# A chunked state-space layer gated with a feed-forward layer: filler tiles, the scan's PSUM copy and the start-up reordered

## Chip, cores and metric

One core of a Trainium2 chip. The metric is the device time in microseconds (us) of one execution. The kernel before takes 337.68 us (median of 4 runs, 336.47 to 340.53). Engines are called as the profile calls them: PE (TensorE), DVE (VectorE), ACT (ScalarE), POOL (GpSimd), SP (SyncE, which issues the transfers here).

## The reference

Two branches read the same x of 2048 rows and 640 columns and are mixed by a gate per row. `A` is a diagonal complex recurrence over 2048 rows with 640 states; `B` is a feed-forward layer with 1728 hidden units.

```python
def _A_ref(x, Lambda_re, Lambda_im, B_re, B_im, C_re, C_im, log_dt, Dskip):
    ...
    Lam_bar = jnp.exp(dt * Lam)
    B_bar = ((Lam_bar - 1.0) / Lam)[:, None] * Bmat
    Bu = jnp.einsum("bld,pd->blp", x + 0j, B_bar)
    ...
    for t in range(L):
        h = Lam_bar[None, :] * h + Bu[:, t, :]
        hs.append(h)
    hseq = jnp.stack(hs, 1)
    y = 2.0 * jnp.einsum("blp,dp->bld", hseq, Cmat).real + x * Dskip[None, None, :]
    return y

def _B_ref(x, w1, w2):
    h = jnp.einsum("bsd,df->bsf", x, w1)
    h = _silu(h)
    return jnp.einsum("bsf,fd->bsd", h, w2)

g = _sigmoid((x * gate_w).sum(-1, keepdims=True))
return g * a + (1 - g) * b
```

## The kernel before

The recurrence is cut into 16 chunks of 128 rows. For chunk c, PE computes `Bu` (U in PSUM) and the gate; DVE multiplies U by decaying powers (`do_V`); PE sums V over time with a triangular matrix (`do_CS`); the sums go to SBUF with the state at the end of the previous chunk (`hpf`) added (`do_CScopy`); DVE multiplies by growing powers (`do_S`), and PE multiplies S by the scaled C matrix (`do_y`). Chunk c needs `hpf` of chunk c-1, so this is a cycle. FFN2 of a chunk (`do_b`) and the hidden tiles of FFN1 (`ffn1_tile`: five matmuls, a sigmoid on ACT, a multiply on DVE) have nothing to do with the cycle and can fill gaps; tiles placed in the loop are called fillers. There are 56 tiles, 14 for each 512 rows.

The PSUM tensor `pbig` has eight banks of 512 columns. CS and y share columns from 2048 on (banks 4 to 6). The narrow FFN2 output (`B2C`, bank 6) shares a bank with the end of CS. The wide FFN2 output is bank 7. In the loop every filler uses bank 0.

```python
NPRE = 2 * FT                 # 28 tiles before the loop
...
def ffn1_tile(n):
    ...
    pr = (n % 4) if n < NPRE else 0      # bank of the tile
    ...
def do_CScopy(c):
    for t in range(10):
        ...                              # bias: zcol, or hpf of the chunk before
        def fn(a, t=t, bias=bias):
            return a.activation(CSsb[:, 128 * t:128 * (t + 1)],
                                pbig[:, R3C + 128 * t:R3C + 128 * (t + 1)],
                                ACTF.Identity, bias=bias)
        ...
# start-up: transfers in the order  x (5), w1 (1), B (10), w2 (2), C (10),
# then the parameter vectors and matrices on DVE, mixed with tiles,
# then the scaling of C (10 on ACT, 10 on DVE) mixed with tiles, then:
do_Bu(0); ...; do_V(0); tiles(2); do_CS(0); do_CScopy(0); do_S(0)
tiles(NPRE)
...
for c in range(NCH):
    fl = list(filler.get(c, []))         # chunks 4 to 11: 4, 3, 4, 3, ... tiles
    if c + 1 < NCH:
        do_Bu(c + 1); do_gate(c + 1); do_Ucopy(c + 1); do_gsig(c + 1)
        do_V(c + 1)
    if fl:
        ffn1_tile(fl.pop(0))
    do_b(c); do_t2(c)
    if fl:
        ffn1_tile(fl.pop(0))
    do_y(c); do_t1(c); do_out(c)
    for rest in fl:
        ffn1_tile(rest)
    if c + 1 < NCH:
        do_CS(c + 1); do_CScopy(c + 1); do_S(c + 1)
```

Of the kernel before, what the change touches and what calls it, by code (L numbers as in the profile page):

```python
# [11 lines left out]
D_MOD = 640  # L12
# [7 lines left out]
NPRE = 2 * FT  # L20
# [14 lines left out]
def _ptile(t):  # L35
    if t < 4:
        return t
    if t < 8:
        return t - 4
    return 4  # L40

# [113 lines left out]
def bass_gated_mix__ssm_conv_s5__dense_activation_silu__prompt_kernel(  # L155
# [19 lines left out]
    with ExitStack() as ctx:  # L175
# [11 lines left out]
        CTraw = sb("CTraw", [128, 10, D_MOD], bf16)  # L187
# [23 lines left out]
        T2s = sb("T2s", [128, 2 * P_ST], bf16)  # L211
        hpf = [sb(f"hpf{i}", [128, 10], f32) for i in range(2)]
        zcol = sb("zcol", [128, 1], f32)
# [3 lines left out]
        sig = [sb(f"sig{i}", [128, 512], bf16) for i in range(2)]  # L217
        ident = sb("ident", [128, 128], bf16)
        LT = sb("LT", [128, 128], bf16)
        halfpi = sb("halfpi", [128, 1], f32)  # L220
        stage = sb("stage", [5, 5 * 128], bf16)
# [25 lines left out]
        g_x = _DmaGroup(sem("s_x"), "DMA_x")  # L247
        g_w1 = _DmaGroup(sem("s_w1"), "DMA_w1")
# [20 lines left out]
        for kt in range(KT):  # L269
            dma(xT[:, kt, :], A_x[0, :, kt * 128:(kt + 1) * 128], g_x, writes=["xT"], transpose=True)  # L270
        dma(w1[:, :, :], B_w1[:, :].rearrange("(kt p) f -> p kt f", p=128), g_w1, writes=["w1"])
        for kt in range(KT):
            dma(BT[:, kt, 0:P_ST], A_B_re[:, kt * 128:(kt + 1) * 128], g_bt, writes=["BT"], transpose=True)
            dma(BT[:, kt, P_ST:2 * P_ST], A_B_im[:, kt * 128:(kt + 1) * 128], g_bt, writes=["BT"],
                transpose=True)
        dma(w2[:, 0:FT - 1, :],
            B_w2[0:(FT - 1) * 128, :].rearrange("(kt p) d -> p kt d", p=128), g_w2, writes=["w2"])
        dma(w2[0:64, FT - 1, :], B_w2[(FT - 1) * 128:F_FF, :], g_w2, writes=["w2"])
        for t5 in range(KT):
            dma(CTraw[:, t5, :], A_C_re[:, t5 * 128:(t5 + 1) * 128], g_ct, writes=["CTraw"],  # L280
                transpose=True)
            dma(CTraw[:, KT + t5, :], A_C_im[:, t5 * 128:(t5 + 1) * 128], g_ct, writes=["CTraw"],
                transpose=True)
# [15 lines left out]
        pool(lambda g: g.memset(zcol[:, :], 0.0), writes=["zcol"])  # L299

        def ffn1_tile(n):
# [3 lines left out]
            pr = (n % 4) if n < NPRE else 0  # L305
            pc = 512 * pr
            tok = f"hTp{pr}"
            for kt in range(KT):
# [5 lines left out]
                kw = dict(reads=["w1", "xT"], writes=rb(pc, pc + 512))  # L314
# [5 lines left out]
            def fs(a, rows_f=rows_f, n=n, pc=pc):  # L320
                return a.activation(sig[n % 2][0:rows_f, :], pbig[0:rows_f, pc:pc + 512], ACTF.Sigmoid)  # L321
            S.op(ACT, fs, reads=[tok] + rb(pc, pc + 512), writes=[f"sig{n % 2}"])
            def fm(v, rows_f=rows_f, n=n, buf=buf, ft=ft, pc=pc):
                return v.tensor_tensor(hT[buf][0:rows_f, ft, :], pbig[0:rows_f, pc:pc + 512],  # L324
                                       sig[n % 2][0:rows_f, :], ALU.mult)
            S.op(DVE, fm, reads=[tok, f"sig{n % 2}"] + rb(pc, pc + 512),
# [71 lines left out]
        S.op(DVE, lambda v: v.tensor_copy(Ere[:, :, 0:1], cols[:, I_LRE, 0:KT].unsqueeze(2)),  # L398
             reads=[f"col{I_LRE}"], writes=["Ere"])
        S.op(DVE, lambda v: v.tensor_copy(Eim[:, :, 0:1], cols[:, I_LIM, 0:KT].unsqueeze(2)),  # L400
             reads=[f"col{I_LIM}"], writes=["Eim"])
        S.op(DVE, lambda v: v.tensor_copy(col(I_PRA), col(I_LRE)), reads=[f"col{I_LRE}"], writes=[f"col{I_PRA}"])
        S.op(DVE, lambda v: v.tensor_copy(col(I_PIA), col(I_LIM)), reads=[f"col{I_LIM}"], writes=[f"col{I_PIA}"])
        pcur = [I_PRA, I_PIA]
        pnxt = [I_PRB, I_PIB]

        def e_round(r):
            nonlocal pcur, pnxt
            w = 1 << r
            pre, pim = pcur  # L410
            def fA(v, w=w, pre=pre):
                return v.tensor_tensor(tAb[:, :, 0:w], Ere[:, :, 0:w], bc_col(pre, w), ALU.mult)
            def fB(v, w=w, pim=pim):
                return v.tensor_tensor(tBb[:, :, 0:w], Eim[:, :, 0:w], bc_col(pim, w), ALU.mult)
            def fC(v, w=w, pim=pim):
                return v.tensor_tensor(tCb[:, :, 0:w], Ere[:, :, 0:w], bc_col(pim, w), ALU.mult)
            def fD(v, w=w, pre=pre):
                return v.tensor_tensor(tDb[:, :, 0:w], Eim[:, :, 0:w], bc_col(pre, w), ALU.mult)
# [4 lines left out]
            S.op(DVE, lambda v, w=w: v.tensor_tensor(Ere[:, :, w:2 * w], tAb[:, :, 0:w], tBb[:, :, 0:w], ALU.subtract),  # L423
                 reads=["tA", "tB"], writes=["Ere"])
            S.op(DVE, lambda v, w=w: v.tensor_tensor(Eim[:, :, w:2 * w], tCb[:, :, 0:w], tDb[:, :, 0:w], ALU.add),
                 reads=["tC", "tD"], writes=["Eim"])
            if r < 6:
# [5 lines left out]
                S.op(DVE, lambda v, pin=pin: v.tensor_scalar_mul(col(pin), col(I_DEN), 2.0),  # L433
                     reads=[f"col{I_DEN}"], writes=[f"col{pin}"])
                pcur, pnxt = pnxt, pcur

        for r in range(7):
            e_round(r)

        S.op(DVE, lambda v: v.tensor_copy(Aa[:, 0:4, :], Ere[:, 0:4, :]), reads=["Ere"], writes=["Aa"])  # L440
        S.op(DVE, lambda v: v.tensor_copy(Aa[:, 4:8, :], Ere[:, 0:4, :]), reads=["Ere"], writes=["Aa"])
        S.op(DVE, lambda v: v.tensor_copy(Aa[:, 8, :], Ere[:, 4, :]), reads=["Ere"], writes=["Aa"])
        S.op(DVE, lambda v: v.tensor_copy(Aa[:, 9, :], Ere[:, 4, :]), reads=["Ere"], writes=["Aa"])
        tiles(2)
        S.op(DVE, lambda v: v.tensor_scalar_mul(An[:, 0:4, :], Eim[:, 0:4, :], -1.0), reads=["Eim"], writes=["An"])
        S.op(DVE, lambda v: v.tensor_scalar_mul(An[:, 8, :], Eim[:, 4, :], -1.0), reads=["Eim"], writes=["An"])
        S.op(DVE, lambda v: v.tensor_copy(An[:, 4:8, :], Eim[:, 0:4, :]), reads=["Eim"], writes=["An"])
        S.op(DVE, lambda v: v.tensor_copy(An[:, 9, :], Eim[:, 4, :]), reads=["Eim"], writes=["An"])
        tiles(2)
        S.op(DVE, lambda v: v.tensor_tensor(dd1[:, :, :], Ere[:, :, :], Ere[:, :, :], ALU.mult),  # L450
             reads=["Ere"], writes=["dd1"])
        S.op(DVE, lambda v: v.tensor_tensor(dd2[:, :, :], Eim[:, :, :], Eim[:, :, :], ALU.mult),
             reads=["Eim"], writes=["dd2"])
        tiles(1)
        S.op(DVE, lambda v: v.tensor_tensor(dd3[:, :, :], dd1[:, :, :], dd2[:, :, :], ALU.add),
             reads=["dd1", "dd2"], writes=["dd3"])
        S.op(DVE, lambda v: v.reciprocal(dd1[:, :, :], dd3[:, :, :]), reads=["dd3"], writes=["dd1"])
        tiles(2)
        S.op(DVE, lambda v: v.tensor_tensor(Rre_b[:, :, :], Ere[:, :, :], dd1[:, :, :], ALU.mult),
             reads=["Ere", "dd1"], writes=["Rre_b"])  # L460
        S.op(DVE, lambda v: v.tensor_tensor(Rimn_b[:, :, :], Eim[:, :, :], dd1[:, :, :], ALU.mult),
             reads=["Eim", "dd1"], writes=["Rimn_b"])
        tiles(1)
# [12 lines left out]
        for t in range(10):  # L476
# [11 lines left out]
            if t % 2 == 1:  # L488
                tiles(1)
        for kt in range(KT):  # L490
            def fn(v, kt=kt):
                return v.tensor_scalar(Ddiag[:, kt, :], ident[:, :],
                                       cols[:, I_D, kt:kt + 1], None, ALU.mult)
            S.op(DVE, fn, reads=["ident", f"col{I_D}"], writes=["Ddiag"])
        tiles(2)

        def retile(t5):
            return t5 if t5 < 4 else 8

        def imtile(t5):  # L500
            return t5 + 4 if t5 < 4 else 9

        for t5 in range(KT):
            rt, it = retile(t5), imtile(t5)
            def fa(a, t5=t5):
                return a.activation(T1s[:, 0:D_MOD], CTraw[:, t5, :], ACTF.Copy,
                                    scale=cols[:, I_K2IM, t5:t5 + 1])
            S.op(ACT, fa, reads=["CTraw", f"col{I_K2IM}"], writes=["T1s"])
            def fb(v, t5=t5, it=it):
                return v.scalar_tensor_tensor(CTT[:, it, :], CTraw[:, KT + t5, :],  # L510
                                              cols[:, I_NK2RE, t5:t5 + 1], T1s[:, 0:D_MOD],
                                              ALU.mult, ALU.subtract)
            S.op(DVE, fb, reads=["CTraw", f"col{I_NK2RE}", "T1s"], writes=["CTT"])
            def fc(a, t5=t5):
                return a.activation(T2s[:, 0:D_MOD], CTraw[:, KT + t5, :], ACTF.Copy,
                                    scale=cols[:, I_K2IM, t5:t5 + 1])
            S.op(ACT, fc, reads=["CTraw", f"col{I_K2IM}"], writes=["T2s"])
            def fd(v, t5=t5, rt=rt):
                return v.scalar_tensor_tensor(CTT[:, rt, :], CTraw[:, t5, :],
                                              cols[:, I_K2RE, t5:t5 + 1], T2s[:, 0:D_MOD],  # L520
                                              ALU.mult, ALU.subtract)
            S.op(DVE, fd, reads=["CTraw", f"col{I_K2RE}", "T2s"], writes=["CTT"])
            tiles(2)
# [214 lines left out]
        for c in range(NCH):  # L738
# [7 lines left out]
            if fl:  # L746
                ffn1_tile(fl.pop(0))
            do_b(c)
            do_t2(c)
            if fl:  # L750
                ffn1_tile(fl.pop(0))
# [63 lines left out]
```

## Time and profile before

| | before |
|---|---|
| time, median | 337.68 us |
| span of the profiled run, mean granted clock | 335.2 us, 0.942 |
| start to first y | 87.29 us |
| first y to CS of chunk 4 | 42.32 us |
| chunks 4 to 11 (with fillers) | 149.74 us |
| chunks 12 to 14 (plain) | 38.19 us |
| chunk 15: CS to y | 10.90 us |
| last y to the end | 6.76 us |

The stages come from PE's timeline: they are differences of the start times of the CS and y matmuls, and they add up to the span.

The second is the table of groups (busy us, mean ns of one, then the idle time of the engine ahead of the group and what ended it):

```profile
L310 PE MATMUL pbig<-xT,w 128*128 128x512 bf16 (+1 forms) x280 | 73.5, 409 | 47.1 <-DVE hT L324 26.1
...
L593 ACT ACTIVATE CSsb<-pbig,hpf 128x128 bf16<-128x128 f32 x150 | 55.2, 368 | 10.9 <-PE pbig L577 6.3
```

PE stands idle for 47.1 us ahead of tile matmuls, 26.1 of it ended by a tile's own multiply on DVE. A copy of 128 columns costs 368 ns on ACT. The third is a filler step in which the clock held (columns as in the prediction):

```profile
129.61:148.42 18.81, 15.04 (x108) 7.92 (x109) 8.03 (x14) 8.46 (x19) 0.00 (x0) 1.00 0.05 18
```

The prediction shows a four-filler step of 20.47 us, at clock 0.92. Chunks 4 and 8 have the same waits of 2.20 and 1.57 us but take 18.81 and 18.82 us, at 1.00; in the other six filler steps the clock falls to 0.90 to 0.92.

### The profile page before, as it was taken

How to read it: one execution, taken by the hardware profiler on the slowest of the kernel's cores; microseconds unless marked ns; L12 is line 12 of the kernel's file. 1: busy time of each engine (PE TensorE's matmuls, PEld its weight loads, DVE VectorE, ACT ScalarE, POOL GpSimd, SP SyncE). 2: the span in 40 equal slices, each digit the busy share in tenths (PEclk: the TensorE clock that was granted, in tenths of full speed). 3: DMA queues.
4: the chain of work that ended last, by engine and by line, in shares of the span. 5: the costliest groups of instructions: out<-in, count | busy, mean ns of one | idle time of the engine just before them, and what ended most of it. 6: DMA issues, size and time to landing. Idle time of an engine off the chain costs nothing.

```text
span 335.2 us, 4386 instructions
## 1 busy us (share of the span) xinstructions
PE 251.6 (75%) x1703; PEld 129.4 (39%) x1703; DVE 162.8 (49%) x367; ACT 152.5 (45%) x329; POOL 1.2 (0%) x10
## 2 busy tenths in 40 slices
PE   0019198875887888787988879787978978887855
PEld 0004143332544545343543435343443525544422
DVE  2967978954351642636262351726262352551630
ACT  5004147854266366445362726345362717366342
POOL 1000000000000000000000000000000000000000
PEclk9999789998999999999797979999797979999969
DMA  5997981000000000000000000000000000000000
GB/s 116 205 320 132 299 138 23 4 0 2 0 22 20 0 22 20 2 20 1 11 11 0 22 0 22 0 22 0 20 2 0 20 3 20 3 19 20 3 20 20
DMA packets 28630, 13.22 MB, mean 39 GB/s; under 512 B 24194, under 2 KB 27970, under 8 KB 28610
## 3 DMA queue, kind: packets, MB, share of 16 engines
q1 hardware_dynamic: 28610, 12.95, 15.6%
q8 instruction: 13, 0.21, 0.3%
q14 instruction: 7, 0.06, 0.1%
HBM read 4.43 MB, written 2.62 MB: 21 GB/s over the span
## 4 chain that ended last, share of the span: by engine, by line
PE 38%; ACT 23%; DVE 16%; SPq 14%; issue 6%; DMA 1%; DVEq 0%; ACTq 0%
ACT CSsb L593 18%; SPq L261 13%; PE pbig L621 12%; PE pbig L310 9%; PE pbig L680 8%; DVE hT L324 3%; PE pbig L635 3%; ACT sig L321 3%; PE pbig L691 2%; DVE Ssb L612 2%; DVE T1s L604 2%; PE pbig L577 2%; DVE T1v L563 2%; ACT ta L669 2%; DVE T2s L606 2%
## 5 line engine op out<-in xcount | busy, mean ns | idle before, releaser
L310 PE MATMUL pbig<-xT,w 128*128 128x512 bf16 (+1 forms) x280 | 73.5, 409 | 47.1 <-DVE hT L324 26.1
L680 PE MATMUL pbig<-w,hT 128*128 128x512 bf16 x224 | 69.5, 395 | 0.0
L321 ACT ACTIVATE sig<-pbig 128x512 bf16<-128x512 f32 (+1 forms) x56 | 33.1, 598 | 70.9 <-PE pbig L310 65.9
L593 ACT ACTIVATE CSsb<-pbig,hpf 128x128 bf16<-128x128 f32 x150 | 55.2, 368 | 10.9 <-PE pbig L577 6.3
L310 PEld LDWEIGHTS pbig<-xT,w 128*128 128x128 bf16 (+1 forms) x280 | 26.5, 103 | 81.7 <-issue 26.4
L324 DVE TENSOR_TENSOR hT<-pbig,sig 128x512 bf16<-128x512 f32 (+1 forms) x56 | 37.6, 685 | 41.9 <-ACT sig L321 31.2
L691 PE MATMUL pbig<-w,hT 128*128 128x128 bf16 x224 | 50.5, 225 | 9.9 <-ACT CSsb L593 9.9
L546 PE MATMUL pbig<-BT,xT 128*128 128x512 bf16 (+1 forms) x320 | 46.6, 300 | 5.3 <-DVE hT L324 5.3
L621 PE MATMUL pbig<-CTT,Ssb 128*128 128x512 bf16 x160 | 42.9, 421 | 0.0
L604 DVE TENSOR_TENSOR T1s<-Aa,CSsb 128x1280 bf16<-128x1280 bf16 x16 | 13.2, 826 | 59.5 <-ACT CSsb L593 59.5
L546 PEld LDWEIGHTS pbig<-BT,xT 128*128 128x128 bf16 x320 | 25.2, 98 | 25.5 <-issue 6.7
L680 PEld LDWEIGHTS pbig<-w,hT 128*128 128x128 bf16 x224 | 22.5, 101 | 28.4 <-issue 8.3
L714 DVE TENSOR_TENSOR osb<-ta,tb 128x640 bf16<-128x640 bf16 x16 | 7.9, 493 | 52.6 <-ACT ta L669 52.6
L669 ACT ACTIVATE ta<-pbig,gsb 128x640 bf16<-128x640 f32 x16 | 12.7, 794 | 40.7 <-PE pbig L642 40.7
L704 ACT ACTIVATE tb<-pbig,g1sb 128x512 bf16<-128x512 f32 x16 | 11.0, 688 | 43.3 <-PE pbig L680 43.3
L691 PEld LDWEIGHTS pbig<-w,hT 128*128 128x128 bf16 x224 | 22.2, 101 | 15.3 <-ACT CSsb L593 15.3
L621 PEld LDWEIGHTS pbig<-CTT,Ssb 128*128 128x128 bf16 x160 | 16.7, 109 | 25.1 <-issue 11.0
L559 ACT ACTIVATE Usb<-pbig 128x1280 bf16<-128x1280 f32 x16 | 19.7, 1230 | 6.8 <-PE pbig L649 6.8
L577 PE MATMUL pbig<-LT,Vsb 128*128 128x128 bf16 x160 | 11.6, 219 | 7.1 <-ACT ta L669 6.8
L563 DVE TENSOR_TENSOR T1v<-Wa,Usb 128x1280 bf16<-128x1280 bf16 x16 | 13.1, 819 | 4.3 <-ACT Usb L559 4.3
L577 PEld LDWEIGHTS pbig<-LT,Vsb 128*128 128x128 bf16 x160 | 9.4, 97 | 11.0 <-issue 7.8
L571 DVE TENSOR_TENSOR Vsb<-T1v,T2v 128x1280 bf16<-128x1280 bf16 x16 | 13.2, 825 | 0.5
(86 smaller groups left out, 170.6 us busy)
## 6 DMA issues: line engine op xcount, KB each, us to landing
out_dram<-osb SPq DMA_DIRECT2D x16, 160.0 KB, 1.8
w<-in_B_w_dram SPq DMA_DIRECT2D x1, 2160.0 KB, 8.6
w<-in_B_w_dram SPq DMA_DIRECT2D x1, 2080.0 KB, 8.9
xT<-in_A_x_dram SPq DMA_TRANSPOSE x5, 5.3
BT<-in_A_B_re_dram SPq DMA_TRANSPOSE x5, 3.8
BT<-in_A_B_im_dram SPq DMA_TRANSPOSE x5, 3.7
w<-in_B_w_dram SPq DMA_DIRECT2D x1, 80.0 KB, 8.6
CTraw<-in_A_C_re_dram SPq DMA_TRANSPOSE x5, 4.0
```

The lines of the kernel that those rows point to most:

```text
L261: return eng.dma_start(out_ap, in_ap, transpose=True)
L310: return pe.matmul(pbig[0:rows_f, pc:pc + 512], lhsT=w1[:, kt, ft * 128:ft * 128 + rows_f], rhs=xT[:, kt, sc * 512:(sc + 1) * 512], start= ...
L321: return a.activation(sig[n % 2][0:rows_f, :], pbig[0:rows_f, pc:pc + 512], ACTF.Sigmoid)
L324: return v.tensor_tensor(hT[buf][0:rows_f, ft, :], pbig[0:rows_f, pc:pc + 512], sig[n % 2][0:rows_f, :], ALU.mult)
L546: return pe.matmul(pbig[:, UC + c0:UC + c1], lhsT=xT[:, kt, c * TCH:(c + 1) * TCH], rhs=BT[:, kt, r0:r1], start=(kt == 0), stop=(kt == KT ...
L563: S.op(DVE, lambda v: v.tensor_tensor(T1v[:, :], Wa[:, :], Usb[:, :], ALU.mult), reads=["Wa", "Usb"], writes=["T1v"])
L577: return pe.matmul(pbig[:, R3C + 128 * t:R3C + 128 * (t + 1)], lhsT=Vsb[:, 128 * t:128 * (t + 1)], rhs=LT[:, :], start=True, stop=True)
L593: return a.activation(CSsb[:, 128 * t:128 * (t + 1)], pbig[:, R3C + 128 * t:R3C + 128 * (t + 1)], ACTF.Identity, bias=bias)
L604: S.op(DVE, lambda v: v.tensor_tensor(T1s[:, :], Aa_flat, CSsb[:, :], ALU.mult), reads=["Aa", "CSsb"], writes=["T1s"])
L621: return pe.matmul(pbig[:, YC:YC + 512], lhsT=Ssb[:, 128 * t:128 * (t + 1)], rhs=CTT[:, t, 0:512], start=(t == 0), stop=False)
L680: return pe.matmul(pbig[:, B1C:B1C + 512], lhsT=hT[buf][0:rows, kt, j * 128:(j + 1) * 128], rhs=w2[0:rows, kt, 0:512], start=(kt == 0), st ...
L691: return pe.matmul(pbig[:, B2C:B2C + 128], lhsT=hT[buf][0:rows, kt, j * 128:(j + 1) * 128], rhs=w2[0:rows, kt, 512:640], start=(kt == 0), ...
```

## The change

It means to do five things: (1) in the loop, queue the first filler's multiply ahead of V and give the third filler bank 7; (2) copy CS with one ACT operation and add `hpf` in ten DVE operations; (3) scale C after S of chunk 0 instead of ahead of chunk 0, in place, pair by pair; (4) load C ahead of w2, and w1 in five pieces between those of x; (5) place 16 tiles in place of 28 before the loop, with three fillers in each of the chunks 0 to 3, and move the set-up of Aa, An and Ddiag from DVE to POOL. A third sigmoid buffer (`sig`) comes with it, and the places of the tiles among the set-up operations move.

```diff
-NPRE = 2 * FT
+NPRE = 16
...
         for kt in range(KT):
-            dma(xT[:, kt, :], A_x[0, :, kt * 128:(kt + 1) * 128], g_x, writes=["xT"], transpose=True)
-        dma(w1[:, :, :], B_w1[:, :].rearrange("(kt p) f -> p kt f", p=128), g_w1, writes=["w1"])
+            dma(xT[:, kt, :], A_x[0, :, kt * 128:(kt + 1) * 128], g_x[kt],
+                writes=[f"xT{kt}"], transpose=True)
+            dma(w1[:, kt, :], B_w1[kt * 128:(kt + 1) * 128, :], g_w1[kt], writes=[f"w1_{kt}"])
...                              (B unchanged; the ten C transposes now stand ahead of w2)
-        def ffn1_tile(n):
+        def ffn1_tile(n, pr=0):
...
-            pr = (n % 4) if n < NPRE else 0
+            if n < NPRE:
+                pr = n % 4
...                              (Aa, An, Ddiag: the same operations on POOL)
         def do_CScopy(c):
-            for t in range(10):
-                ...
-                def fn(a, t=t, bias=bias):
-                    return a.activation(CSsb[:, 128 * t:128 * (t + 1)],
-                                        pbig[:, R3C + 128 * t:R3C + 128 * (t + 1)],
-                                        ACTF.Identity, bias=bias)
+            def fn(a):
+                return a.activation(CSsb[:, :], pbig[:, R3C:R3C + 2 * P_ST], ACTF.Copy)
+            S.op(ACT, fn, reads=["CS"] + rb(R3C, R3C + 2 * P_ST), writes=["CSsb"])
+            if c > 0:
+                hb = hpf[(c - 1) % 2]
+                for t in range(10):
+                    def fa(v, t=t, hb=hb):
+                        return v.tensor_scalar(CSsb[:, 128 * t:128 * (t + 1)],
+                                               CSsb[:, 128 * t:128 * (t + 1)],
+                                               hb[:, t:t + 1], None, ALU.add)
+                    S.op(DVE, fa, reads=["CSsb", f"hpf{(c - 1) % 2}"], writes=["CSsb"])
...
         do_S(0)
+        tiles(2)
+
+        for k in range(KT):      (scaling of C, two ACT and two DVE operations for each k)
+            ...
+            tiles(2)
+
         tiles(NPRE)
...
         for c in range(NCH):
             fl = list(filler.get(c, []))
+            fa_ = fl[0:1]
+            fb_ = fl[1:2]
+            fcd = fl[2:4]
+            if c > 0:
+                do_CS(c)
+                do_CScopy(c)
+                do_S(c)
             if c + 1 < NCH:
                 do_Bu(c + 1)
                 do_gate(c + 1)
                 do_Ucopy(c + 1)
                 do_gsig(c + 1)
+            for t_ in fa_:
+                ffn1_tile(t_, pr=0)
+            if c + 1 < NCH:
                 do_V(c + 1)
-            if fl:
-                ffn1_tile(fl.pop(0))
             do_b(c)
             do_t2(c)
-            if fl:
-                ffn1_tile(fl.pop(0))
+            for t_ in fb_:
+                ffn1_tile(t_, pr=0)
             do_y(c)
             do_t1(c)
             do_out(c)
-            for rest in fl:
-                ffn1_tile(rest)
-            if c + 1 < NCH:
-                do_CS(c + 1)
-                do_CScopy(c + 1)
-                do_S(c + 1)
+            for i, t_ in enumerate(fcd):
+                ffn1_tile(t_, pr=(7 if i == 0 else 0))
```

## The prediction

> **What bounds the kernel now.** I read the page first: shares of the engines, the 40 slices, the chain.
>
> ```profile
> span 335.2 us, 4386 instructions
> ...
> PE 251.6 (75%) x1703; PEld 129.4 (39%) x1703; DVE 162.8 (49%) x367; ACT 152.5 (45%) x329; POOL 1.2 (0%) x10
> ...
> PE   0019198875887888787988879787978978887855
> ...
> PEclk9999789998999999999797979999797979999969
> ```
>
> TensorE is the busiest engine, yet it does nothing for about 24 us at the start, has half-empty slices after that, and in the second half its granted clock falls to 0.7 again and again. So the span splits into a start-up, and a loop over 16 chunks (I call one chunk a step, measured from its CS matmuls, L577, to the next). The windows view, cut at those matmuls, gives the loop (columns: window, length, then busy us and count of PE, PEld, DVE, ACT, POOL, then granted clock, DMA share, GB/s):
>
> ```profile
> 116.89:129.61 12.72, 10.74 (x88) 6.11 (x89) 5.65 (x11) 6.78 (x16) 0.00 (x0) 1.00 0.05 14
> ...
> 166.10:186.57 20.47, 16.70 (x110) 8.32 (x110) 8.78 (x15) 9.02 (x20) 0.00 (x0) 0.92 0.05 17
> 186.57:204.44 17.87, 15.67 (x104) 7.87 (x103) 7.41 (x13) 8.42 (x19) 0.00 (x0) 0.90 0.00 0
> ...
> 317.54:328.44 10.90, 7.05 (x38) 3.44 (x39) 3.10 (x6) 3.67 (x10) 0.00 (x0) 0.69 0.04 15
> ```
>
> A step without FFN filler tiles takes 12.72 us, one with four 20.47, one with three 17.87: a filler costs about 1.8 us, although its five matmuls start 0.216 us apart (1.08 us). TensorE's own timeline says why:
>
> ```profile
> 174.53 0.22 PE L691 MATMUL pbig<-w,hT 64*128 64x128 bf16 x1
> 176.95 2.29 PE L310 MATMUL pbig<-xT,w 128*128 128x512 bf16 x5 [2.20 <-DVE hT L324]
> 179.03 2.97 PE L621 MATMUL pbig<-CTT,Ssb 128*128 128x512 bf16 x10
> ...
> 182.67 1.24 PE L310 MATMUL pbig<-xT,w 128*128 128x512 bf16 x5
> 185.49 1.24 PE L310 MATMUL pbig<-xT,w 128*128 128x512 bf16 x5 [1.57 <-DVE hT L324]
> ```
>
> The second filler shares PSUM bank 0 with the first, so it waits for the first one's VectorE multiply, which is queued behind the V operations; the fourth waits for the third in the same way. After the 2.20 us gap the filler takes 2.29 us in place of 1.24: the clock has dropped. Bookkeeping: PE work of a four-filler step 14.87 (next part) + 2.20 + 1.57 + slow matmuls (2.29-1.08) + (2.76-2.16) = 20.4; measured 20.47. The waits view confirms the two waits of the loop:
>
> ```profile
> PE pbig L310 <- DVE hT L324: 26.1, 15, 2.2
> ...
> PE pbig L691 <- ACT CSsb L593: 9.9, 7, 3.8
> ```
>
> The second is the narrow FFN2 output, which lies in a bank of the CS result and so waits for all ten CS copies: 1.00 us in a plain step, 3.85 us in the last. The start-up, last, from ScalarE's and TensorE's timelines:
>
> ```profile
> 52.66 0.83 ACT L506 ACTIVATE T1s<-CTraw,cols 128x640 bf16<-128x640 bf16 x1 [1.19 <-DMA CTraw<-in_A_C_im_dram]
> ...
> 64.89 2.32 PE L546 MATMUL pbig<-BT,xT 128*128 128x512 bf16 x10 [0.59 <-DVE hT L324]
> ...
> 87.29 2.33 PE L621 MATMUL pbig<-CTT,Ssb 128*128 128x512 bf16 x10
> ```
>
> The C matrices land last (52.6 us); their scaling, mixed with FFN tiles, stands in front of everything of chunk 0, and the first y starts only at 87.3.
>
> **What the Trainium skill says.** "TensorE: Matmul & The Clock Gate", Part 1, has the array's clock halved after about one idle window of 3.4 us and full again after about as long busy. The trace agrees in size (granted clock 0.50 in 176.95 to 180.00) but 2.20 us of idleness is enough here; 1.57 is not. "ScalarE: Activation LUTs", section What ACT_TABLE_LOAD costs, gives 186 ns + 0.833 ns per element, 93 ns more for a per-partition operand. That is 387 ns for a 128-wide copy with bias and 1252 ns for one of 1280; the trace has 368 and 1230 (the U copy). "VectorE: DVE Perf Modes", section on the TRN2 errata, says small SBUF operations pay a fixed cost each; its formula would give under 100 ns for 128 bf16 elements, but the trace's operation of exactly this form (the D-diagonal, a per-column scalar) takes 254 ns. I use the trace. "SBUF — State Buffer", section Who interferes with whom, lets a VectorE operation with two SBUF inputs and a GpSimd read block one another; POOL has 1.2 us here, so nothing in this trace shows it.
>
> **The change part by part.** *Fillers.* The first filler's multiply now stands before V; the third goes to bank 7. PE work from dense windows: CS 0.55, Bu 2.72, gate 0.13, FFN2 4.0 with its small gaps, call it 4.15, y 3.0, filler 1.08 each. Sum: 10.55 + 1.08 per filler, that is 14.87 with four, 13.79 with three. Is anything later than PE? From a CS start, four-filler step: CS done 0.75, one copy to 2.0, ten adds (below) to 4.95, S 2.61 to 7.6, first multiply to 8.3. PE reaches the second filler at 8.6: just free. Bank 7 is free (FFN2 was evacuated during y). V ends near 11, needed at 13.8. So both waits go, and with them the cold clock. Steps 4 to 11 took 149.8 us (129.61 to 279.42); now 4 x 14.87 + 4 x 13.79 = 114.6. **Minus 35.2.** I allow 0.2 us in each of the 12 filler steps for the thin margin: plus 2.4.
>
> *CS copy.* Ten copies at 0.40 us pitch (4.0) become one of 1.23 plus ten VectorE adds. The five D-diagonal operations start 50.0 to 51.1, 0.29 apart, each waiting for the one before as the adds will: 2.9. The sum is 4.1: the path to S is no shorter; ScalarE loses 2.8 us a step and VectorE gains 2.9. What goes is FFN2's 1.00 us wait. A plain step: y starts at max(PE 7.65, S 7.6) instead of 8.65, and the rest (4.08) stays: 11.75 against 12.72, three steps, **minus 2.9**. Step 15: y starts 7.7 after its CS in place of 10.9, **minus 3.2**.
>
> *Start-up.* Only 16 tiles before the loop, the C scaling after S of chunk 0, C loaded before w2, x and w1 interleaved. The queue: transposes of 640 rows cost 1.27 us each, of x 2.5; w1 and w2 each slowed the transposes behind them by 3.4 to 3.8. B ends at about 34, lands near 37; C's last issue moves from 49.3 to about 46, so C lands at 49 rather than 52.6. Bu(0), 64.9 before, starts at about 37 to 38; U copy 1.3, V 2.6, CS 0.75, copy 1.25, S 2.6 with waits: S(0) at 49 to 50. Then the C scaling on VectorE, ten at 0.89 plus four multiplies at 0.6: 11.3 from about 50.5, done near 62. FFN2 of chunk 0 runs to about 64 at a partly cold clock, one filler, y(0) at **66** against 87.3. **Minus 21.3.** GpSimd takes Aa, An and the D-diagonal off VectorE, 3.3 us, but may block the dd operations for up to 2 us; counted as nil.
>
> *Moved work.* Twelve tiles come into steps 0 to 3: one after y(0), 1.1; then three steps of 13.79 in place of 12.72, 3.2. **Plus 4.3.**
>
> Sum: 335.2 - 35.2 + 2.4 - 2.9 - 3.2 - 21.3 + 4.3 = 279.3 span. The timed run of this profile was 336.97, 1.8 above its span: 281, of which I take off 1 as B and C may flow a little faster: **280**.
>
> **Rivals.** (1) The adds become the path: the same CS chain, now on VectorE, also delays the first multiply and keeps the bank-0 wait. For it: 0.3 us margin only. Against: 0.29 us pitch in the trace. If an add costs 0.4, each filler step pays about 1.1 more and plain steps 1.1: 280 becomes 297. (2) The start-up gain is hidden: the SP queue has the same transposes, and C lands only 3 to 4 us earlier; the twelve tiles merely move. For it: the queue is issuing without pause to 50.6. Against: chunk 0 no longer waits for C. If y(0) came at 78, 292. (3) FFN tiles in the loop keep costing 1.8 us each, through some other bank wait: 37 x 0.7 more in steps 1 to 11, about 306. (4) The prologue overlaps better than by my count (a warm clock, C at 46): 272.
>
> **Range and chances.** The step bookkeeping closes within 0.1 us on two steps, so the loop is the firmer half; start-up is good to some 6 us. All rivals that lose still leave over 10% of gain. 270 to 293; faster 0.97, same 0.02, slower 0.01.
>
> **What would show it.** Right: step windows of 14 to 15 us with clock 1.00; no wait of L310 for the hT multiply in the loop; no wait of the narrow FFN2 for CSsb but in the last step; ten adds in about 2.9 us; y(0) near 66. Wrong: steps at 16 or more with gaps before fillers or y (adds), y(0) after 72 (start-up), or a granted clock below 0.95 in dense steps.

## More of the kernel before

Besides the views that the prediction shows, three are useful. The first is the chain that ended last, on the page; it gives shares of the span by engine and then by line.

```profile
PE 38%; ACT 23%; DVE 16%; SPq 14%; issue 6%; DMA 1%; DVEq 0%; ACTq 0%
ACT CSsb L593 18%; SPq L261 13%; PE pbig L621 12%; PE pbig L310 9%; PE pbig L680 8%; DVE hT L324 3%; PE pbig L635 3%; ACT sig L321 3%; PE pbig L691 2%; DVE Ssb L612 2%; DVE T1s L604 2%; PE pbig L577 2%; DVE T1v L563 2%; ACT ta L669 2%; DVE T2s L606 2%
```

PE is on the chain for 38% only, though it is busy for 75% of the span; the ten copies of CS on ACT (L593) alone are 18%.

## The result

The changed kernel takes 276.15 us (median of 11 runs, 275.15 to 278.98) against 337.35 us of the kernel before in the same rounds (16 runs). The ratio is 0.818, 95% interval 0.8154 to 0.8205. Ratios here are the mean time of one kernel's fast runs over that of the other's of the same rounds, so they are not quite the ratio of the medians quoted.

| stage | before, us | after, us | difference | predicted |
|---|---|---|---|---|
| start to first y | 87.29 | 65.43 | -21.86 | -21.3 |
| first y to CS of chunk 4 (ten of the twelve moved tiles) | 42.32 | 45.40 | +3.08 | +4.3 |
| chunks 4 to 11 | 149.74 | 114.06 | -35.68 | -35.2 + 2.4 |
| chunks 12 to 14 | 38.19 | 35.23 | -2.96 | -2.9 |
| chunk 15, CS to y | 10.90 | 7.60 | -3.30 | -3.2 |
| last y to the end | 6.76 | 6.78 | +0.02 | 0 |
| span | 335.2 | 274.5 | -60.7 | -55.9 |

The other two of the twelve tiles, the first two fillers of chunk 0, come before its y (PE starts them at 59.26 and 64.34).

The page of the kernel after, with the lines that answer to those of before (span, busy shares, PE and its clock in 40 slices, the chain by engine):

```profile
span 274.5 us, 4365 instructions
...
PE 235.9 (86%) x1703; PEld 126.0 (46%) x1703; DVE 197.6 (72%) x504; ACT 114.7 (42%) x185; POOL 10.4 (4%) x23
...
PE   0115977589999999999999999999999999898864
...
PEclk9999999979999999999999999999999999999999
...
PE 69%; SPq 11%; DVE 10%; ACT 6%; issue 2%; DMA 1%; ACTq 0%; DVEq 0%
```

Once the loop runs, PE has no half-empty slice before the last and the clock stays up; PE is now 69% of the chain instead of 38%. The windows view, cut at the CS matmuls (columns as in the prediction), for a four-filler step, a three-filler step, a plain step and the last:

```profile
110.83:125.57 14.74, 14.74 (x109) 8.08 (x109) 10.50 (x25) 6.72 (x11) 0.00 (x0) 1.00 0.04 12
125.57:139.28 13.71, 13.71 (x105) 7.51 (x104) 10.23 (x24) 6.09 (x10) 0.00 (x0) 1.00 0.04 14
...
224.89:236.65 11.76, 10.65 (x90) 6.13 (x90) 8.74 (x22) 5.04 (x8) 0.00 (x0) 1.00 0.04 14
260.12:267.72 7.60, 4.80 (x39) 2.58 (x39) 5.50 (x16) 2.29 (x3) 0.00 (x0) 1.00 0.06 22
```

In a filler step PE's busy time equals the length of the step: 14.74 of 14.74 us. PE is the bound there. In a plain step 1.1 us is free. The timeline of PE and DVE within the three-filler step shows how close the first filler's multiply comes:

```profile
127.60 2.87 DVE L572 TENSOR_SCALAR CSsb<-CSsb,hpf 128x128 bf16<-128x128 bf16 x10 [0.44 <-ACT CSsb L566]
...
133.23 0.69 DVE L331 TENSOR_TENSOR hT<-pbig,sig 128x512 bf16<-128x512 f32 x1
...
134.06 1.24 PE L317 MATMUL pbig<-xT,w 128*128 128x512 bf16 x5
...
135.14 2.32 PE L599 MATMUL pbig<-CTT,Ssb 128*128 128x512 bf16 x10
```

The ten adds take 2.87 us. The first filler's multiply ends at 133.92 and the second filler, which needs that bank, starts at 134.06 with no bracket, that is with no wait that the profile reports. The 0.14 us between are no reserve: where PE does wait for such a multiply, the same 0.13 to 0.15 us pass (kernel before: end at 176.82, start at 176.95; with V put first, below: 150.42 and 150.57). PE reaches the filler just as the bank comes free; it starts 0.16 us after the last FFN2 matmul (133.90), against 0.15 in chunk 0 (64.19 to 64.34), where the bank is long free. So at most 0.01 us is lost. The waits view has, of the loop and of the first steps:

```profile
PE pbig L555 <- ACT ta L647: 2.9, 3, 1.0
...
PE pbig L669 <- ACT CSsb L566: 1.1, 1, 1.1
...
PE pbig L317 <- DVE hT L331: 0.5, 1, 0.5
```

26.1 us of waits of tiles for their multiplies became 0.5 us in the start-up; the wait of the narrow FFN2 for the CS copies, 9.9 us, is 1.1 in the last step. What is left in the loop is that CS waits 1.0 us for ACT to read y's row (`ta`), in the three plain steps. In the start-up, from the same timeline:

```profile
36.26 2.89 PE L524 MATMUL pbig<-BT,xT 128*128 128x512 bf16 x20 [1.49 <-DMA BT<-in_A_B_im_dram]
...
49.03 0.83 ACT L711 ACTIVATE T2v<-CTT,cols 128x640 bf16<-128x640 bf16 x1 [2.15 <-DMA CTT<-in_A_C_im_dram]
...
65.43 2.32 PE L599 MATMUL pbig<-CTT,Ssb 128*128 128x512 bf16 x10
```

Bu of chunk 0 starts when B has landed; C lands at 49.0; the scaling on DVE runs from 50.70 to 61.76; y of chunk 0 starts at 65.43, right behind the filler ahead of it. So its start is set by PE's order from Bu of chunk 1 on (53.84, after a wait of 2.48 us for a tile's multiply), and not by the end of the scaling.

### The profile page after: what moved, and what is told of

Its sections match the earlier page's. It is cut to its first block, busy times and chain, and to the rows that moved or that the text cites. A ratio compares the mean times of both kernels' runs of the same rounds, so it can differ in the third digit from the quotient of the medians.

```text
span 274.5 us, 4365 instructions
## 1 busy us (share of the span) xinstructions
PE 235.9 (86%) x1703; PEld 126.0 (46%) x1703; DVE 197.6 (72%) x504; ACT 114.7 (42%) x185; POOL 10.4 (4%) x23
## 4 chain that ended last, share of the span: by engine, by line
PE 69%; SPq 11%; DVE 10%; ACT 6%; issue 2%; DMA 1%; ACTq 0%; DVEq 0%
PE pbig L317 16%; PE pbig L658 14%; PE pbig L524 13%; PE pbig L599 13%; SPq L265 10%; DVE CSsb L572 4%; PE pbig L555 4%; PE pbig L669 3%; PE pbig L613 3%; ACT CSsb L566 2%; SPq L266 2%; DVE Ssb L590 2%; DVE T1s L582 2%; PE pbig L607 1%; DMA BT<-in_A_B_im_dram 1%
## 5 line engine op out<-in xcount | busy, mean ns | idle before, releaser
L317 PE MATMUL pbig<-xT,w 128*128 128x512 bf16 (+1 forms) x280 | 70.9, 390 | 18.6 <-DMA w<-in_B_w_dram 17.8
L658 PE MATMUL pbig<-w,hT 128*128 128x512 bf16 x224 | 64.3, 379 | 0.0
L524 PE MATMUL pbig<-BT,xT 128*128 128x512 bf16 (+1 forms) x320 | 47.6, 305 | 5.1 <-DVE hT L331 2.5
L669 PE MATMUL pbig<-w,hT 128*128 128x128 bf16 x224 | 49.0, 219 | 1.1 <-ACT CSsb L566 1.1
L572 DVE TENSOR_SCALAR CSsb<-CSsb,hpf 128x128 bf16<-128x128 bf16 x150 | 38.2, 255 | 15.6 <-ACT CSsb L566 10.8
L317 PEld LDWEIGHTS pbig<-xT,w 128*128 128x128 bf16 (+1 forms) x280 | 25.0, 100 | 49.4 <-DMA w<-in_B_w_dram 19.9
L599 PE MATMUL pbig<-CTT,Ssb 128*128 128x512 bf16 x160 | 37.2, 379 | 2.1 <-DVE Ssb L590 1.7
L658 PEld LDWEIGHTS pbig<-w,hT 128*128 128x128 bf16 x224 | 21.8, 97 | 28.2 <-issue 4.2
L599 PEld LDWEIGHTS pbig<-CTT,Ssb 128*128 128x128 bf16 x160 | 15.3, 98 | 21.3 <-DVE Ssb L590 3.4
L669 PEld LDWEIGHTS pbig<-w,hT 128*128 128x128 bf16 x224 | 21.8, 98 | 2.9 <-ACT CSsb L566 1.4
L566 ACT ACTIVATE CSsb<-pbig 128x1280 bf16<-128x1280 f32 x16 | 19.8, 1237 | 4.6 <-PE pbig L555 4.3
```

The costliest lines, as they stand in the source:

```text
L317: return pe.matmul(pbig[0:rows_f, pc:pc + 512], lhsT=w1[:, kt, ft * 128:ft * 128 + rows_f], rhs=xT[:, kt, sc * 512:(sc + 1) * 512], start= ...
L524: return pe.matmul(pbig[:, UC + c0:UC + c1], lhsT=xT[:, kt, c * TCH:(c + 1) * TCH], rhs=BT[:, kt, r0:r1], start=(kt == 0), stop=(kt == KT ...
L566: return a.activation(CSsb[:, :], pbig[:, R3C:R3C + 2 * P_ST], ACTF.Copy)
L572: return v.tensor_scalar(CSsb[:, 128 * t:128 * (t + 1)], CSsb[:, 128 * t:128 * (t + 1)], hb[:, t:t + 1], None, ALU.add)
L599: return pe.matmul(pbig[:, YC:YC + 512], lhsT=Ssb[:, 128 * t:128 * (t + 1)], rhs=CTT[:, _cslot(t), 0:512], start=(t == 0), stop=False)
L658: return pe.matmul(pbig[:, B1C:B1C + 512], lhsT=hT[buf][0:rows, kt, j * 128:(j + 1) * 128], rhs=w2[0:rows, kt, 0:512], start=(kt == 0), st ...
```

## The experiments

Theory: the loop gain is the two bank waits and the cold clock they cause, removed by order and by bank 7; the copy form matters only where no filler stands ahead of FFN2; the start-up gain is the order (scaling of C behind chunk 0, C ahead of w2). Rivals: the gain comes mostly from the copy form; or from the finer transfers and POOL's help. All variants below start from the kernel after, except one that starts from the kernel before. Three batches ran, each with its own runs of the kernel before (medians 337.68, 337.50 and 337.45), so I compare ratios; the kernel after has 0.818. The variants give correct results.

### The order of V and the first filler's multiply

```diff
-            for t_ in fa_:
-                ffn1_tile(t_, pr=0)
             if c + 1 < NCH:
                 do_V(c + 1)
+            for t_ in fa_:
+                ffn1_tile(t_, pr=0)
```

> The changed kernel with one thing undone: V of the next chunk is again queued before the first filler's multiply. Theory (the place in VectorE's queue sets when bank 0 comes free): in each of the 12 steps with fillers the multiply ends at about 11.0 us instead of 8.3 after the step's CS, TensorE is there at 8.5, so it waits 2.5 us, and in most steps it comes back at half clock, 1 to 2 us more. 276 becomes 306 if the clock holds, up to 323 if it drops in every step. Rival (the place does not matter once ScalarE is relieved of the ten copies): within 2 us of 276.

Measured: 313.41 us (2 runs), ratio 0.9276 (0.9212 to 0.9341), clock 0.956. Its steps 1 to 11 take 16.16 to 18.93 us in place of 13.70 to 14.74; plain steps stay at 11.74. In its waits view:

```profile
PE pbig L317 <- DVE hT L331: 27.8, 13, 2.5
```

The swap of two neighbouring pieces of the program is worth 37 us, 35.6 of them in steps 1 to 11 (190.89 against 155.33). This is not quite the gain of the filler steps: chunks 4 to 11 alone take 140.50 here, 26.4 more than after but 9.2 less than before, and steps 1 to 3, 9 us of the loss, had no fillers in the kernel before. The parts overlap; each undoing is measured with the others in place.

### Bank 7 for the third filler

```diff
-                ffn1_tile(t_, pr=(7 if i == 0 else 0))
+                ffn1_tile(t_, pr=0)
```

> The changed kernel with bank 7 not used: third and fourth filler both in bank 0. Theory: only the four steps with four fillers pay, each the 1.57 us wait of the kernel before, without a drop of the clock: 276 becomes 282.5, the four-filler steps 16.3 instead of 14.7, the three-filler steps stay 13.7. Rival (the second bank is the larger half of the loop's gain, since every filler step gets it): all 12 steps longer, 290 or more.

Measured: 282.54 us (4 runs), ratio 0.8371 (0.8331 to 0.8411). Only the four-filler steps change: 16.46 to 16.48 us against 14.72 to 14.74, 1.74 us each. Its waits view:

```profile
PE pbig L317 <- DVE hT L331: 6.8, 5, 1.6
```

With three fillers bank 0 has been read out by the time that the third comes; with four, the fourth waits 1.6 us. The clock stays up through gaps of that length (1.00 in chunks 4 to 7).

### Order and bank alone, on the kernel before

```diff
                 do_gsig(c + 1)
-                do_V(c + 1)
             if fl:
                 ffn1_tile(fl.pop(0))
+            if c + 1 < NCH:
+                do_V(c + 1)
...
-            for rest in fl:
-                ffn1_tile(rest)
+            for i, rest in enumerate(fl):
+                ffn1_tile(rest, pr=(7 if i == 0 else 0))
```

> The kernel before with only the loop's order changed: first filler's multiply before V, third filler in bank 7. Start-up and the ten ScalarE copies stay. Theory: steps 4 to 11 go from 149.8 us to about 114 (14.7 with four, 13.7 with three), all else stays: 337.4 becomes about 301. Rival (the copies on ScalarE keep half of the waits): 315 or more, with gaps left before the fillers.

Measured: 301.56 us (2 runs), ratio 0.8926 (0.887 to 0.8981). Its steps 4 to 11 take 114.8 us in all (149.74 before, 114.06 after), with the copy form and the start-up of before. So these few lines alone, with neither the new copy nor the new start-up, give the filler term of the sum. The CS matmuls that bound its first four-filler and its first three-filler step:

```profile
130.00 0.72 PE L578 MATMUL pbig<-LT,Vsb 128*128 128x128 bf16 x10 [0.97 <-ACT ta L670]
...
144.82 0.72 PE L578 MATMUL pbig<-LT,Vsb 128*128 128x128 bf16 x10
...
158.62 0.72 PE L578 MATMUL pbig<-LT,Vsb 128*128 128x128 bf16 x10
```

Its plain steps stay at 12.72 to 12.74.

### The old copy form

The kernel after with `do_CScopy` of the kernel before (ten ACT copies with bias, no adds).

```diff
-                return a.activation(CSsb[:, :], pbig[:, R3C:R3C + 2 * P_ST], ACTF.Copy)
+                    return a.activation(CSsb[:, 128 * t:128 * (t + 1)],
+                                        pbig[:, R3C + 128 * t:R3C + 128 * (t + 1)],
+                                        ACTF.Identity, bias=bias)
```

> The changed kernel with the CS copy in its old form: ten ScalarE copies with bias in place of one copy and ten VectorE adds. Theory (both forms take 4.1 us to S; what the new one gains is the bank that the narrow FFN2 output shares with CS): steps with fillers stay within 0.3 us of 13.7 and 14.7, the three plain steps go from 11.74 to 12.7, the last from 7.6 to 10.9 before y: 276 becomes 282 to 284. Rival (taking 2.8 us a step off ScalarE is what freed the loop): filler steps grow by 1 us or more, 292 or more.

Measured: 282.56 us (4 runs), ratio 0.8361 (0.832 to 0.8401). Filler steps lengthen by 0.08 to 0.10 us only, plain steps by 0.98 to 0.99 (12.72 to 12.74), and the last step's y starts 10.67 us after its CS. PE's timeline in the last step:

```profile
268.79 0.29 PE L670 MATMUL pbig<-w,hT 128*128 128x128 bf16 x1 [3.85 <-ACT CSsb L571]
```

The one copy is worth 6 to 7 us, all but 1 of them in the last four chunks, where no filler stands between CS and FFN2. It is not a cheaper copy: DVE's 2.87 us of adds take the place of ACT's time. What goes is the wait of the narrow FFN2 for a bank that the slow copies hold.

### w2 ahead of C

```diff
+        dma(w2[:, 0:FT - 1, :], ...)
+        dma(w2[0:64, FT - 1, :], ...)
         for t5 in range(KT):
             dma(CTT[:, t5, :], A_C_re[...], ...)
...
-        dma(w2[:, 0:FT - 1, :], ...)
-        dma(w2[0:64, FT - 1, :], ...)
```

> The changed kernel with w2 put back in front of the C matrices in the queue. Theory (C's landing, 49.0 us, sets when the C scaling and with it y of chunk 0 starts): w2 costs 1.5 us of issue and slows the transposes behind it by some 3.4, so C lands near 54 and y(0) moves from 65.4 to about 70: 276 becomes 280 to 281. Rival (the place in the queue is hidden behind chunk 0's chain): less than 1 us.

Measured: 281.14 us (4 runs), ratio 0.8334 (0.8304 to 0.8365). The steps of the loop are the same to 0.02 us; the first y moves from 65.43 to 69.53. The first three C transposes behind w2 take 2.91, 2.56 and 2.37 us in place of 1.27, and DVE waits for the scaling input, which here comes 4.7 us later than in the kernel after (50.70):

```profile
55.43 0.88 DVE L719 SCALAR_TENSOR_TENSOR CTT<-CTT,cols,T2v 128x640 bf16<-128x640 bf16 x1 [7.00 <-ACT ctmp L715]
```

### The scaling of C ahead of chunk 0

The block that scales C moved from behind `do_S(0)` to ahead of `do_Bu(0)`, as before; all else as after.

```diff
+        for k in range(KT):       (the scaling block)
+            ...
         do_Bu(0)
         do_gate(0)
...
         do_S(0)
         tiles(2)
-        for k in range(KT):       (the scaling block)
-            ...
```

> The changed kernel with the C scaling back in front of chunk 0 (Bu, U, V, CS, S), its loads as changed. Theory (the gain of the start-up is that chunk 0's chain of 12 us runs while C is still loading): Bu(0) starts near 60 instead of 36, S(0) ends near 71 instead of 48, y(0) at about 76 instead of 65.4: 276 becomes 286 to 288. Rival (C's landing alone rules, the order of the two is indifferent): 279 or less.

Measured: 290.05 us (4 runs), ratio 0.8595 (0.8565 to 0.8626): 14 us more than after, somewhat above the range that I gave. The scaling runs from 50.20 to 64.0, and only then V of chunk 0 starts:

```profile
52.75 6.70 PE L317 MATMUL pbig<-xT,w 128*128 128x512 bf16 x20 [13.21 <-DVE hT L331]
...
65.11 0.82 DVE L541 TENSOR_TENSOR T1v<-Wa,Usb 128x1280 bf16<-128x1280 bf16 x1 [1.11 <-ACT Usb L537]
```

The first y comes at 78.71, 13.3 us later. The hold-up passes through two queues: DVE stands for 13.20 us at its first scaling operation, which waits for C; the tiles' multiplies queued behind it come late, so PE stands for 13.21 us at the next tile, and Bu of chunk 0, queued behind the tiles, starts at 59.28 instead of 36.26.

### All 28 tiles before the loop

```diff
-NPRE = 16
+NPRE = 2 * FT
```

> All 28 hidden tiles that FFN1 makes before or in the first chunks are placed before the loop (none left as fillers of steps 0 to 3). My theory: the kt-by-kt start-up fills TensorE only while w1 pieces arrive, so moving twelve more tiles there costs what they cost densely, some 10 us, while steps 1 to 3 fall from 13.7 to 11.7 (6 us in all) and step 0 gives back a few; total 276 to 281, y(0) later than 65.4 by 0 to 10 us. Rival (the tiles would be free in the idle TensorE time of the start-up): y(0) stays at 65 to 66 and the time falls to 269 to 272.

Measured: 280.82 us (4 runs), ratio 0.8323 (0.8287 to 0.836). Steps 1 to 3 fall to 11.74, together 6.05 us less, but y of chunk 0 starts later by 10.4 us, at the far end of what I had given:

```profile
75.80 2.33 PE L599 MATMUL pbig<-CTT,Ssb 128*128 128x512 bf16 x10
```

In its timeline between 52 and 68 the tiles come in pairs, each pair waiting for multiplies that are queued between the scaling operations on DVE. The tiles are not free in the start-up. The kernel after has 18 tiles ahead of its first y, this variant 28. Held against each other, the ten tiles cost the kernel after 6.05 us in the loop, all in steps 1 to 3 (from the first y to the next CS both take 4.13 to 4.14 us); in the start-up they cost 10.4.

### w1 in one transfer

```diff
-            dma(w1[:, kt, :], B_w1[kt * 128:(kt + 1) * 128, :], g_w1[kt], writes=[f"w1_{kt}"])
+        dma(w1[:, :, :], B_w1[:, :].rearrange("(kt p) f -> p kt f", p=128), g_w1[0],
+            writes=[f"w1_{k}" for k in range(KT)])
```

> The changed kernel with w1 in one transfer after x, as before. Theory (the interleaving is neutral: the first tile ends 1 us earlier with it, but B and C are issued 1.5 us later): 275 to 276. Rival (pieces of w1 between the x transposes are what starts the tiles early): 278 or more.

Measured: 274.11 us (4 runs, 273.73 to 276.42), ratio 0.8147 (0.8098 to 0.8197), at or just below the low end of what I expected. Cut into pieces, w1 brings the first sigmoid only 0.55 us earlier (24.95 in the kernel after, 25.50 here), and it holds the transposes back: the last issue of C starts at 46.09 in the kernel after and at 45.35 here. The first y comes 2.2 us earlier here (63.23), but 1.34 us of that is the clock: the last 15 matmuls of Bu of chunk 1 take 1.80 us here and 3.14 in the kernel after, behind the same idle times (2.47 and 2.48 us ahead of Bu, 1.07 within it). First the kernel after, then this one:

```profile
56.15 3.14 PE L524 MATMUL pbig<-BT,xT 128*128 128x512 bf16 x15 [1.07 <-ACT T1v L711]
```

```profile
55.30 1.80 PE L525 MATMUL pbig<-BT,xT 128*128 128x512 bf16 x15 [1.07 <-ACT T1v L712]
```

The intervals overlap, so this part of the change is neutral at best.

### The set-up back on VectorE

```diff
-        pool(lambda g: g.tensor_copy(Aa[:, 0:4, :], Ere[:, 0:4, :]), reads=["Ere"], writes=["Aa"])
+        S.op(DVE, lambda g: g.tensor_copy(Aa[:, 0:4, :], Ere[:, 0:4, :]), reads=["Ere"], writes=["Aa"])
...                              (the rest of Aa, An and Ddiag too, An and Ddiag in their forms of before)
```

> The changed kernel with Aa, An and the D diagonal back on VectorE. Theory (most of it lies in VectorE's idle time before V(0), and POOL's reads cost the dd and R operations 0.9 us anyway): the R operations end 1.8 us later, S(0) about 50, but the scaling is released by C, not by S(0): 276 becomes 276.5 to 277.5. Rival (the off-loaded 2.6 + 1.4 us are on the path): 279 or more.

Measured: 276.45 us (4 runs), ratio 0.8197 (0.8136 to 0.8258): the same time. One DVE operation in the kernel after, while POOL reads SBUF, and then the same operation here:

```profile
22.25 1.11 DVE L460 TENSOR_TENSOR dd<-dd 128x640 f32<-128x640 f32 x1
```

```profile
24.70 0.82 DVE L460 TENSOR_TENSOR dd<-dd 128x640 f32<-128x640 f32 x1
```

POOL's help slows what DVE does beside it, and POOL waits too (its first copy of Aa took 2.28 us, the next of the same shape 1.09). And the vector chain is not what sets the first y: here the last of that chain starts 1.97 us later (30.49 against 28.52), and y no later (63.70). Its two runs at a clock of 1.0 took 274.51 and 274.88 us, its two at 0.981 took 278.02 and 278.40: with nothing changed, 3.5 us go with the clock. Only the run of 274.51 was kept as a trace, so where the clock fell in the others isn't shown. This scatter is larger than what the parts called neutral here could be worth.

### Three attempts to go further

(a) One semaphore for each pair of C transposes, so that the first pair is scaled as soon as it is there.

```diff
-        g_ct = _DmaGroup(sem("s_ct"), "DMA_ct")
+        g_ct = [_DmaGroup(sem(f"s_ct{i}"), f"DMA_ct{i}") for i in range(KT)]
...
         do_CScopy(0)
+        c_act(0)                  (the ACT half of the scaling of pair 0)
         do_S(0)
+        c_dve(0)                  (its DVE half)
```

> One semaphore for each pair of C transposes, so that the scaling of the first pair starts when that pair is there. Theory: the scaling on VectorE starts right behind S(0) at about 48.2 instead of 50.7, y(0) at about 63 instead of 65.4: 273 to 275. Rival: TensorE's own order up to y(0) (Bu(1), FFN2(0)) binds and the time stays within 0.5 of 276.

Measured: 274.39 us (4 runs, 274.29 to 274.98), ratio 0.8135 (0.8104 to 0.8166). The time lies in the range that I gave, but the mechanism is not what I said. The scaling does start at 47.83 in place of 50.70, yet Bu of chunk 1 starts when it did before (53.89 against 53.84):

```profile
53.89 1.24 PE L524 MATMUL pbig<-BT,xT 128*128 128x512 bf16 x5 [1.18 <-ACT sig L328]
...
56.20 1.80 PE L524 MATMUL pbig<-BT,xT 128*128 128x512 bf16 x15 [1.07 <-DVE hT L331]
```

Bu's result lies in banks 1 to 3, which the tiles before the loop use as well, and the multiply of the tile that holds the bank, queued between scaling operations on DVE, ends at 53.74 (the profile names a sigmoid that ends only 0.02 us before Bu starts; in the kernel after it names the multiply). From there on PE's order (Bu, FFN2, a filler, y) sets the first y, as the rival had it. y of chunk 0 is 1.3 us earlier (64.13) because Bu's last 15 matmuls ran warm (1.80 us against 3.14). All four runs lie below the lowest of the kernel after (275.15), at clocks of 0.991 to 1.0, but the intervals of the ratios overlap. It has the lowest ratio that I have, next to that of w1 in one transfer (0.8147). A gain of 1 to 2 us over the kernel after is possible, not shown: the set-up variant gets as far by its clock alone.

(b) The five pieces of w1 issued from ACT's queue at the very start, so that SP has five issues less.

```diff
+            dma(w1[:, kt, :], ..., g_w1[kt], writes=[f"w1_{kt}"], eng=ACT)
+        for kt in range(KT):
             dma(xT[:, kt, :], ...)
-            dma(w1[:, kt, :], ..., g_w1[kt], writes=[f"w1_{kt}"])
```

> The w1 pieces are issued from ScalarE's queue instead of between the transposing loads on SyncE's. Theory: the queue of issues that brings C in gets some 3 us shorter, C lands at 46 instead of 49, the scaling and y(0) follow by 1 to 3 us: 273.5 to 275.5. Rival (the start-up is bound by the chunk-0 chain and not by C's arrival): unchanged at 276.

Measured: 277.04, 277.45 and 277.04 us in three runs, ratio 0.8214 (0.8178 to 0.825): no gain, the expectation fell. The fourth run, the profiled one, took 1377.93 us; in its trace PE's tile matmuls take 1663 ns each in place of some 390, at a recorded clock of 1.0, and the other engines' durations are as ever. It is in no ratio. I have no cause for it.

(c) Both, and in chunks 12 to 14 the gate and the two narrow groups of Bu issued ahead of CS, to fill the 1.0 us in which CS waits.

```diff
+            early = c >= 12 and c + 1 < NCH
+            if early:
+                do_gate(c + 1)
+                do_Bu(c + 1, (2, 3), None)
             if c > 0:
                 do_CS(c)
...
+            if early:
+                do_Bu(c + 1, (0, 1), 1)
```

> Both of the above, and in the last steps the gate of the next chunk and the two narrow groups of Bu are issued ahead of CS, which should take the 1.0 us wait on ScalarE's row out of three plain steps (11.74 to about 11.0 each). If the three gains add: 270 to 272; if the two start-up gains overlap, 272 to 274.

Measured: 280.77 us (6 runs, 279.82 to 281.16), ratio 0.8315 (0.8288 to 0.8343): slower than the kernel after. The trace shows two reasons. First, the start-up. From SP's and PE's timelines:

```profile
2.57 18.72 SPq L265 DMA_TRANSPOSE xT<-in_A_x_dram  x5
```

```profile
7.05 0.29 PE L349 MATMUL pbig<-ident,stage 5*128 5x5 bf16 x5 [7.05 <-DMA stage<-in_gate_w_dram]
```

The five x transposes took 12.42 us in the kernel before and 15.05 in the kernel after (1.64 + 3.96 + 3.20 + 3.28 + 2.97, with w1 pieces between); with w1 issued beside them they take 18.72. And the five small parameter vectors, issued at the same time as w1's pieces (0.8 to 3.2 us), land at 7.05 instead of 3.75 us, so that the whole parameter chain, and CS of chunk 0 (46.88 against 42.99 in variant (a)), come later. In variant (b)'s odd run they land at 6.94 too. Why variant (b) loses only 1 us by this and not 4 isn't shown, as its only trace is of the odd run.

Second, the plain steps remain 11.74 to 11.75 us. In place of the 1.0 us wait there is now a 0.29 us one in two of the three, and another ahead of y:

```profile
237.38 2.33 PE L600 MATMUL pbig<-CTT,Ssb 128*128 128x512 bf16 x10 [0.82 <-DVE Ssb L591]
```

So a plain step is bound by the cycle itself: from CS to y 7.60 us of CS, copy, adds and S, whatever PE has left to do, and from y to the next CS the rest. That last part ends with ACT's reading of y (`ta`): the next CS waits for it because CS and y share banks, not because of `hpf`. No run gives them separate banks. PE's work had only been moved out of one gap into the next. The issue of the narrow groups ahead of the first CS made the step ahead of it 0.7 us longer (14.56).

## Why the prediction was right

The time was 276.15 against 280.0, in the range, and the mechanisms held where the runs test them.

**Fillers.** Four- and three-filler steps of 14.87 and 13.79 were predicted; 14.72 to 14.74 and 13.71 to 13.86 came, at clock 1.00, and the sum of chunks 4 to 11 was 114.06 against 114.6. The bookkeeping of PE work was 0.14 us too long where it took FFN2's 4.0 and said "call it 4.15": the four-filler steps fit with 4.0 (14.73 less 10.72 of the other terms). The three-filler steps then come out at 13.64, 0.07 and 0.22 below what was measured; the 13.86 belongs to steps whose last tile has 64 rows, and the rest is open. The fourth filler waited for another reason than the prediction gives: its wait of 1.57 us is the third's own sigmoid and multiply (0.60 and 0.69 us, with the hand-overs), with no V ahead of them, so bank 7 removes it and the order doesn't.

The variant on the kernel before shows that order and bank do it alone. The mis-sized term is the 2.4 us "for the thin margin": PE reached the second filler just as its bank came free, and lost at most 0.01 us. The margin was even thinner than the 0.3 us stated, but a margin that holds costs nothing, and the schedule repeats from step to step (14.72 to 14.74), so it held each time. Of the 4.8 us by which the span was shorter than the sum, this and the 0.5 us of FFN2 are 2.9, the moved tiles 1.2 and the first y 0.6; the 1 us that the prediction took off at the end made up for 1 of it.

**The CS copy.** Ten adds were to take 2.9 us and took 2.87; the plain step was to be 11.75 and was 11.74; the last step's y was to come at 7.7 us and came at 7.60. The old form, put back, returned the wait of 3.85 us and plain steps of 12.72 to 12.74. The prediction took PE (7.65) and S (7.6) to reach y together; variant (c) shows that S is the firm one of the two. Both parts of the old step were misread by 0.07 us, with opposite signs: y stood 8.58 us after CS, not 8.65, and 4.14 to 4.15 us remained, not 4.08.

**Start-up.** y of chunk 0 was to come at 66 and came at 65.43; Bu at 37 to 38, it came at 36.26; C was to land at 49, it landed at 49.0; the scaling was to end near 62, it ended at 62 to within 0.3. Undoing the parts one at a time moves the first y by 13.3 us (scaling ahead), 4.1 (w2 ahead) and 10.4 us (28 tiles). They sum to more than the 21.86 gained: they overlap, and cannot be booked separately.

**Moved work.** 4.3 us was predicted, 3.08 came. The failing term is the 1.1 us for the tile behind the first y: from y to the next CS there were 4.15 us in the kernel before, without a filler, and 4.13 with one. Without a filler CS waits about 1 us there for ACT to read y (0.98 in the next step of the kernel before); the tile lies in that gap.

**Set-up and w1.** POOL's help was "counted as nil", which the variant without it confirms, with a caveat: the blocking is there. "SBUF — State Buffer", section Who interferes with whom, of the Trainium skill, of which the prediction could only say that no trace showed it, agrees now: 1.11 us against 0.82 for the same two-input operation with and without POOL reading, and 2.28 us against 1.09 for POOL's own copy. Interleaving x and w1, to which the prediction gave no term of its own, gives no gain.

**Rivals.** The adds as path (297): refuted, ten adds take 2.87 us and the filler steps have no wait. The start-up gain hidden (292): refuted. Fillers that keep costing 1.8 us (306): this is nearly what the swapped order of V gives, 313, so it was the right thing to fear. A better overlap with a warm clock (272): not in the kernel after, whose clock was 0.72 from 54 to 60 us, behind the gap of 2.48 us ahead of Bu of chunk 1; the profiled runs in which it stayed at 0.998 or 1.0 took 274.0 to 275.0 us.

## What to carry to other kernels

When two producers share one engine's queue, ask which of their consumers is waiting for a buffer: undoing the move of one short multiply ahead of V's four operations costs 37 us here, and taking away the spare PSUM bank 6. Put work that depends on the last transfer behind everything that doesn't, and measure where filler work is cheap: ten tiles cost 6 us in the loop and 10 in a start-up whose engine merely looked idle. Where a loop-carried cycle sets the step, filling one gap of a busy engine only moves the gap.

## What the Trainium skill lacked or had wrong

- "TensorE: Matmul & The Clock Gate", Part 1, names one idle window of some 3.4 us. In the kernel before an idle time of 2.20 us was followed by a lower clock in six of eight filler steps (0.90 to 0.92 over the step) and not in the two others (1.00). In the kernel after one of 2.48 us, with 1.07 us more behind it, was followed by 0.72 from 54 to 60 us, while the same gaps in the variant with w1 in one transfer, and gaps of 1.6 us in the one-bank variant, were not. So from 2.2 us on a drop can come and need not; between 1.6 and 2.2 us nothing was measured.
- The same part says that the records of the gate are not always to be trusted. One run here is in line with that, though its cause isn't known: 1377.93 us, with tile matmuls of 1663 ns at a recorded clock of 1.0.
- "VectorE: DVE Perf Modes", section on the TRN2 errata: its formula gives under 100 ns, an estimate, for a `tensor_scalar` of 128 bf16 columns. The page says itself that the formula falls short and that the fixed term is about 150 cycles, which gives some 190 ns, again an estimate. With a per-partition operand it took 254 ns, and 0.29 us from one to the next where each waits for the one before.
- "DMA: Bandwidth & Descriptors", section Issuing engines are not separate DMA queues, agrees with what was seen: w1 issued from a second engine did not run for free but lengthened five x transposes to 18.72 us, from 12.42 in the kernel before. Lacking is what a plain transfer costs the transposes behind it: 1.27 us became 2.91, 2.56 and 2.37 us behind w2.
